# RWKV attention with two MLP blocks on one core: a prologue with one reciprocal table, a later broadcast of u, and other PSUM banks for the first chunks

## The chip, the cores and the metric

The kernel runs on one core of one Trainium2 chip. The metric is the device time of one execution in microseconds (us); lower is better. Three timed runs of the kernel before gave 740.57, 743.58 and 743.90 us, so the median is 743.58 us.

## The reference

Three stages follow one another on fp32 data: a linear attention with a decaying state (4 batches, 8 heads, 768 steps, head width 48), an MLP with squared ReLU (3072 tokens, 384 to 2048 to 384), and an MLP with a softmax-weighted activation, a layer norm and a projection (384 to 1024 to 384).

```python
for t in range(S):                       # S = 768, per batch and head
    cur = outer(u * k[t], v[t])          # 48 x 48
    y[t] = r[t] @ (state + cur)
    state = w[:, None] * state + outer(k[t], v[t])

x = y as (3072, 384)
h = maximum(x @ w_in, 0);   x = (h * h) @ w_out
h = x @ w2_in;  solu = h * softmax(h)
out = (solu - mean) / sqrt(var + 1e-6) * g_ln @ w2_out
```

## The kernel before

**Attention in chunks.** The 3072 tokens are cut into 24 chunks of 128; chunk c belongs to batch c % 4. Inside a chunk the recurrence is a masked matrix of scores. The decay is folded in by a table `pt` of powers of w from w^-64 to w^63 (`setup_tables`, L276): r is multiplied with the table, k with the table reversed, and then TensorE (PE) forms scores (L417), VectorE (DVE) copies the part above the diagonal into a tile `atw` (L466), whose diagonal GpSimd (POOL) has already filled from r, u and k (`prep_b`, L370 to L389), and PE multiplies with v (L533). The result y of the first four chunks stays in a PSUM bank until `split_x` (L553) turns it into a high part `xh` (ScalarE, ACT, L563) and a low part `xl` (DVE, L564).

**Split matmuls.** Every fp32 product of the two MLPs is done as three fp32r products: high by high, low by high, high by low. So each weight is split on chip after it has landed in a staging tile `stg`: three DVE instructions undo a 64-bit form (L584, L587, L590), ACT casts the high part (L602), POOL subtracts to get the low part (L603). There are 28 such units for the first MLP and six staging buffers.

**The first MLP.** A step is one tile of 128 hidden units: `p1` (L637) makes it from xh, xl and wih, wil in one of the banks 3 and 4, ACT squares it (L649 to L651), DVE makes the low part gl (L652), and `p2` (L655) adds it, through woh and wol, into the accumulators in banks 5, 6 and 7. A block is 512 tokens, that is four chunks; the first block is begun in halves of 256 tokens (steps 0 to 3 for chunks 0 and 1, steps 4 to 7 for chunks 2 and 3).

**The prologue.** Loads are issued by SyncE (SP) in program order (L825 to L834), with u, broadcast to 128 partitions, issued by ACT (L826). Then `setup_tables`, the first two chunks (L837 to L847), chunks 2 and 3 (L849 to L855), and `setup_ktab` (L317), which transposes two tables by PE through bank 7. The list `YB` at L836 says which bank each of the first chunks' y uses: 5, 6, 7 and 1. The scores of chunks 0, 2 and 3 go to banks 0 and 1, those of chunk 1 to banks 3 and 4.

**What sets the order.** A scheduler that simulates the program fixes the order of instructions on every engine; from then on each engine works through its own list in order and waits on semaphores. So an edit in the prologue also reorders later instructions. The program has eight completion semaphores for its loads, used in turn: the ninth load is issued when the first has landed.

Of the kernel before, what the change touches and what calls it, by code (L numbers as in the profile page):

```python
# [177 lines left out]
def rwkv_moe_moe2_kernel(ctx, tc, rkd, tok, tk2, wd, w, u, w_in, w_out, w2_in, w2_out, g_ln, out):  # L178
# [29 lines left out]
    pwr = ac.tile([GR, 8, NP], F32, name="pwr")  # L208
    ipw = ac.tile([GR, 8, NP], F32, name="ipw")
    kpt = ac.tile([128, DM], F32, name="kpt")  # L210
# [64 lines left out]

    def setup_tables():  # L276
        R = pt[:, 0]
        nc.vector.memset(R[:, :, HC:HC + 1], 1.0)
        nc.vector.tensor_scalar(out=pwr[:, 0], in0=wdt, scalar1=W_MIN, scalar2=W_MAX, op0=ALU.max, op1=ALU.min)
        n, s = 1, 0  # L280
        while n <= HC:
            if n < HC:
                nc.vector.tensor_tensor(out=pwr[:, s + 1], in0=pwr[:, s], in1=pwr[:, s], op=ALU.mult)
            nc.vector.reciprocal(ipw[:, s], pwr[:, s])
            if n == HC:
                nc.vector.tensor_copy(R[:, :, 0], ipw[:, s])
            else:
                for o, src, t in ((HC + n, HC, pwr), (HC + 1 - 2 * n, HC + 1 - n, ipw)):
                    nc.vector.tensor_tensor(
                        out=R[:, :, o:o + n],  # L290
                        in0=R[:, :, src:src + n],
                        in1=t[:, s].unsqueeze(2).to_broadcast([GR, NP, n]),
                        op=ALU.mult,
                    )
            n, s = 2 * n, s + 1
        nc.scalar.copy(pt[:, 1], R[:, :, ::-1])

# [19 lines left out]
    def setup_ktab():  # L317
        v = ps[:, 7, :].rearrange("p (a b) -> p a b", a=NP)
        for p in range(NP):
# [20 lines left out]
    def halves(t):  # L340
        return t.rearrange("q p (s i) -> q p s i", s=2)

    def prep_rk(c, eng=None):
        if c >= B:
            k = halves(rk_t[c])
            nc.gpsimd.tensor_tensor(out=k, in0=k, in1=sub_tab(pt[:, 1]), op=ALU.mult)
            for j in range(2):
                q = slice(RO[j], RO[j] + D)
                r = halves(mv[c % 2][q, j])
                nc.gpsimd.tensor_tensor(out=r, in0=r, in1=sub_tab(pt[q, 0]), op=ALU.mult)  # L350
        elif eng:
            eng.tensor_tensor(out=rk_t[c], in0=rk_t[c], in1=pt, op=ALU.mult)
        else:
            for p in range(0, NP, 2):
                for i, t in enumerate((pt[:, 0], pt[:, 0, :, ::-1])):
                    x = rk_t[c][:, i, p:p + 2]
                    nc.vector.tensor_tensor(out=x, in0=x, in1=t[:, p:p + 2], op=ALU.mult)
# [53 lines left out]

    def pe_scores(c, sb=0):
        rk = rk_t[c]
        if c < B:
            for h in range(H):
                o = RO[h % 2]
# [44 lines left out]

    def dve_mask(c, sb=0):
        if c < B:
            m = mask.bitcast(U32).unsqueeze(1).to_broadcast([C, NP, C])
            for i in range(2):
                nc.vector.copy_predicated(  # L466
# [358 lines left out]
    nc.sync.dma_start(out=wdt, in_=wd)  # L825
    nc.scalar.dma_start(out=ub, in_=u.unsqueeze(0).to_broadcast([128, DM]))  # L826
    load_chunk(0)
    w1_load()
    load_chunk(1)
# [5 lines left out]
    setup_tables()  # L835
    SB, YB = (0, 3, 0, 0), (5, 6, 7, 1)  # L836
    for c in range(2):  # L837
# [10 lines left out]
    setup_wm()  # L848
    for c in range(2, 4):  # L849
        prep_rk(c, nc.gpsimd)  # L850
        prep_b(c)
        pe_scores(c, SB[c])
        dve_mask(c, SB[c])
        pe_av_direct(c, YB[c])
        split_x(c)  # L855
    setup_ktab()
# [169 lines left out]
```

## Time and profile before

| | |
|---|---|
| Median of three runs | 743.58 us |
| Profiled execution, its own time | 740.04 us |
| Its span | 738.2 us |
| PE busy in the span | 707.3 us (96%) |
| DVE busy | 417.5 us (57%) |
| ACT, POOL busy | 322.1 us (44%), 268.2 us (36%) |
| Granted TensorE clock, mean | 0.984 of full speed |
| DMA | 62.72 MB, 85 GB/s mean |

The profile is of one execution, taken by the hardware profiler. Times in it count from the start of the span. A group of instructions is named by its engine, its line in the kernel, its operation, and output and inputs by tile name. "Idle before" is time in which the engine stood still just before the instruction, with what ended it behind an arrow. PE's two clock levels are 2.4 GHz (granted 1.00) and 1.2 GHz (granted 0.50). Most fp32 matmuls appear as two entries where they take two passes.

### The profile page before, as it was taken

What the parts mean: (1) busy time and instruction counts of PE and PEld (TensorE: products, weight loads), DVE (VectorE), ACT (ScalarE), POOL (GpSimd) and SP (SyncE); (2) the same over time, 40 slices, a digit from 0 to 9 for tenths busy, and PEclk for the clock granted to TensorE, in tenths of its full rate; (3) what the DMA queues carried; (4) which work ended last, traced back from release to release, by engine and by line L of the source; (5) the groups of instructions that cost most, each with busy time, mean ns of one, the idle gap of its engine ahead of it and who ended that gap; (6) DMA issues with size and microseconds to landing.
All of it is one profiled execution on the core that took longest, in us unless ns stands there. A gap on an engine that the chain in (4) does not pass through costs nothing.

```text
span 738.2 us, 13162 instructions
## 1 busy us (share of the span) xinstructions
PE 707.3 (96%) x5088; PEld 604.3 (82%) x5088; DVE 417.5 (57%) x764; ACT 322.1 (44%) x625; POOL 268.2 (36%) x297
## 2 busy tenths in 40 slices
PE   2699999899999999999999999999999999999996
PEld 2579777688888888888888888888899999999996
DVE  6879997444643333333332265714777767677771
ACT  1325566344545454544555455644424232322232
POOL 4978777515543333333332021722213120200000
PEclk9869999999999999999999999999999999999999
DMA  9946553313223222322143015320210100000001
GB/s 258 268 132 226 178 179 91 95 36 99 84 66 110 62 61 64 109 67 68 46 120 115 12 25 192 109 86 1 96 65 17 67 15 21 22 22 23 21 33 37
DMA packets 35112, 62.72 MB, mean 85 GB/s; under 512 B 7777, under 2 KB 17378, under 8 KB 35042
## 3 DMA queue, kind: packets, MB, share of 16 engines
q1 hardware_dynamic: 34898, 61.60, 27.0%
q8 instruction: 42, 0.69, 0.4%
q10 hardware_dynamic: 144, 0.20, 0.3%
q14 instruction: 28, 0.23, 0.1%
HBM read 48.41 MB, written 9.44 MB: 78 GB/s over the span
## 4 chain that ended last, share of the span: by engine, by line
PE 82%; DVE 6%; DMA 3%; issue 2%; POOL 2%; SPq 2%; ACT 2%; DVEq 0%; ACTq 0%; POOLq 0%
PE ps L644 8%; PE ps L645 8%; PE ps L662 7%; PE ps L663 7%; PE ps L646 7%; PE ps L666 7%; PE ps L812 5%; PE ps L811 5%; PE ps L814 5%; PE ps L748 4%; PE ps L750 4%; PE ps L749 4%; PE ps L795 3%; PE ps L507 2%; PE ps L430 2%
## 5 line engine op out<-in xcount | busy, mean ns | idle before, releaser
L652 DVE TENSOR_TENSOR gl<-ps,gh 128x512 fp32r<-128x512 f32 (+1 forms) x100 | 66.7, 667 | 173.6 <-ACT gh L651 173.5
L644 PE MATMUL ps<-xh,wih 128*128 128x512 f32 (+1 forms) x300 | 118.3, 396 | 3.8 <-ACT xh L563 2.1
L646 PE MATMUL ps<-xh,wil 128*128 128x512 f32 (+1 forms) x300 | 115.9, 387 | 2.7 <-POOL wil L603 2.7
L662 PE MATMUL ps<-gh,woh 128*128 128x512 f32 (+1 forms) x300 | 115.0, 386 | 1.4 <-ACT gh L651 1.4
L645 PE MATMUL ps<-xl,wih 128*128 128x512 f32 (+1 forms) x300 | 115.7, 386 | 0.5 <-DVE xl L564 0.5
L663 PE MATMUL ps<-gh,wol 128*128 128x512 f32 (+1 forms) x300 | 114.2, 383 | 0.3 <-POOL wol L603 0.3
L649 ACT ACTIVATE ps<-ps 128x512 f32<-128x512 f32 (+1 forms) x100 | 56.4, 565 | 115.9 <-PE ps L646 115.8
L350 POOL TENSOR_TENSOR mv<-mv,pt 48x512 f32<-48x512 f32 x40 | 52.8, 1321 | 90.2 <-DMA mv<-in_rkd_dram 89.8
L666 PE MATMUL ps<-gl,woh 128*128 128x512 f32 (+1 forms) x300 | 84.1, 383 | 0.4 <-DVE gl L652 0.4
L644 PEld LDWEIGHTS ps<-xh,wih 128*128 128x128 f32 x300 | 57.3, 191 | 16.4 <-ACT xh L563 2.4
L646 PEld LDWEIGHTS ps<-xh,wil 128*128 128x128 f32 x300 | 57.4, 192 | 14.3 <-POOL wil L603 2.9
L662 PEld LDWEIGHTS ps<-gh,woh 128*128 128x128 f32 x300 | 56.9, 190 | 13.4 <-ACT gh L651 2.0
L645 PEld LDWEIGHTS ps<-xl,wih 128*128 128x128 f32 x300 | 57.5, 192 | 11.3 <-DVE xl L564 1.2
L663 PEld LDWEIGHTS ps<-gh,wol 128*128 128x128 f32 x300 | 56.7, 190 | 11.6 <-POOL wol L603 0.5
L666 PEld LDWEIGHTS ps<-gl,woh 128*128 128x128 f32 x300 | 55.8, 190 | 11.7 <-DVE gl L652 0.9
L811 PE MATMUL ps<-w2oh,lth 128*128 128x384 f32 x192 | 65.1, 339 | 0.2 <-ACT lth L804 0.2
L812 PE MATMUL ps<-w2ol,lth 128*128 128x384 f32 x192 | 65.1, 339 | 0.0
L651 ACT CAST gh<-ps 128x512 fp32r<-128x512 f32 (+1 forms) x100 | 57.2, 572 | 4.3 <-PE ps L663 1.4
L650 ACT ACTIVATE ps<-ps 128x512 f32<-128x512 f32 (+1 forms) x100 | 56.5, 566 | 2.9
L748 PE MATMUL ps<-w2ih,xh 128*128 128x512 f32 x144 | 57.3, 398 | 0.0
L749 PE MATMUL ps<-w2il,xh 128*128 128x512 f32 x144 | 56.8, 395 | 0.0
L750 PE MATMUL ps<-w2ih,xl 128*128 128x512 f32 x144 | 56.7, 395 | 0.0
(121 smaller groups left out, 1192.3 us busy)
## 6 DMA issues: line engine op xcount, KB each, us to landing
stg<-in_w_in_dram SPq DMA_DIRECT2D x18, 512.0 KB, 5.9
stg<-in_w_out_dram SPq DMA_DIRECT2D x24, 384.0 KB, 3.7
tok<-in_tk_dram SPq DMA_DIRECT2D x20, 384.0 KB, 3.7
x2d<-stg SPq DMA_DIRECT2D x18, 256.0 KB, 2.5
x2r<-x2d SPq DMA_DIRECT2D x6, 768.0 KB, 5.0
out_dram<-ob SPq DMA_DIRECT2D x24, 192.0 KB, 1.9
kd<-in_rkd_dram SPq DMA_DIRECT2D x20, 224.0 KB, 3.8
mv<-in_rkd_dram SPq DMA_DIRECT2D x40, 96.0 KB, 2.3
```

The lines of the kernel that those rows point to most:

```text
L644: nc.tensor.matmul(hp, wih[g][:, k, f], xh[:, k, cs], start=(k == 0), stop=False)
L645: nc.tensor.matmul(hp, wih[g][:, k, f], xl[:, k, cs], start=False, stop=False)
L646: nc.tensor.matmul(hp, wil[g][:, k, f], xh[:, k, cs], start=False, stop=(k == KD - 1))
L652: nc.vector.tensor_tensor(out=gl, in0=hp, in1=gh.bitcast(F32), op=ALU.subtract)
L662: nc.tensor.matmul(acc[e], woh[m // 4][:, m % 4, f], gh, start=start, stop=False)
L663: nc.tensor.matmul(acc[e], wol[m // 4][:, m % 4, f], gh, start=False, stop=False)
L666: nc.tensor.matmul(acc[e], woh[m // 4][:, m % 4, f], gl, start=False, stop=stop)
L748: nc.tensor.matmul(o, x2h[j][:, k, s], w2["ih"][:, k, fs], start=(k == 0), stop=False)
L749: nc.tensor.matmul(o, x2h[j][:, k, s], w2["il"][:, k, fs], start=False, stop=False)
L750: nc.tensor.matmul(o, x2l[j][:, k, s], w2["ih"][:, k, fs], start=False, stop=(k == KD - 1))
L811: nc.tensor.matmul(o, hi[:, m], w2["oh"][:, m], start=(m == 0), stop=False)
L812: nc.tensor.matmul(o, hi[:, m], w2["ol"][m // 4][:, m % 4], start=False, stop=False)
```

## The change

Four things in the prologue are changed, and one tile goes.

1. The broadcast of u is issued by SP behind the two loads of chunk 0, not by ACT beside the first load.
2. The powers of w: the positive powers are still doubled step by step, but the negative ones are no longer built beside them from seven small reciprocals. Instead the whole negative half is one reciprocal of the positive half read backwards (63 powers of 4 head pairs), behind one of 4 elements.
3. The outputs y of chunks 2 and 3 move from banks 7 and 1 to banks 1 and 0, and the table transposes of `setup_ktab` from bank 7 to bank 1. Chunk 3's scores and masking are issued in two halves (even heads in bank 0, odd heads in bank 1), and chunk 2's output stands between them.
4. Chunks 2 and 3 are prepared together ahead of both chunks' scores, and POOL's table products for chunks 4 and 5 may not come before the last instruction of that preparation (`after_first`).

```diff
 def setup_tables():
-        while n <= HC:
-            if n < HC:
-                nc.vector.tensor_tensor(out=pwr[:, s + 1], in0=pwr[:, s], in1=pwr[:, s], op=ALU.mult)
-            nc.vector.reciprocal(ipw[:, s], pwr[:, s])
-            if n == HC:
-                nc.vector.tensor_copy(R[:, :, 0], ipw[:, s])
-            else:
-                for o, src, t in ((HC + n, HC, pwr), (HC + 1 - 2 * n, HC + 1 - n, ipw)):
...
+        while n < HC:
+            nc.vector.tensor_tensor(out=pwr[:, s + 1], in0=pwr[:, s], in1=pwr[:, s], op=ALU.mult)
+            nc.vector.tensor_tensor(
+                out=R[:, :, HC + n:HC + 2 * n],
+                in0=R[:, :, HC:HC + n],
+                in1=pwr[:, s].unsqueeze(2).to_broadcast([GR, NP, n]),
+                op=ALU.mult,
+            )
             n, s = 2 * n, s + 1
+        nc.vector.reciprocal(R[:, :, 0], pwr[:, s])
+        nc.vector.reciprocal(R[:, :, 1:HC], R[:, :, :HC:-1])

 def setup_ktab():
-        v = ps[:, 7, :].rearrange("p (a b) -> p a b", a=NP)
+        v = ps[:, 1, :].rearrange("p (a b) -> p a b", a=NP)

+    def after_first(c):
+        if c < B + 2:
+            tc.add_manual_dep(
+                nc.cur_bb.bb.instructions[-1], last_first.name,
+                mybir.DependencyInfo(mybir.DependencyClass.NoSync, mybir.DependencyReason.DATA),
+                reason="after_first",
+            )
 def prep_rk(c, eng=None):        # after_first(c) behind each of its three POOL products
...
-    nc.scalar.dma_start(out=ub, in_=u.unsqueeze(0).to_broadcast([128, DM]))
     load_chunk(0)
+    nc.sync.dma_start(out=ub, in_=u.unsqueeze(0).to_broadcast([128, DM]))
...
-    SB, YB = (0, 3, 0, 0), (5, 6, 7, 1)
+    SB, YB = (0, 3, 0, 0), (5, 6, 1, 0)
...
-    for c in range(2, 4):
-        prep_rk(c, nc.gpsimd)
-        prep_b(c)
-        pe_scores(c, SB[c])
-        dve_mask(c, SB[c])
-        pe_av_direct(c, YB[c])
-        split_x(c)
+    prep_rk(2, nc.gpsimd)
+    prep_b(2)
+    prep_rk(3, nc.gpsimd)
+    prep_b(3)
+    last_first = nc.cur_bb.bb.instructions[-1]
+    pe_scores(2)
+    dve_mask(2)
+    pe_scores(3, 0, range(0, H, 2))
+    pe_av_direct(2, YB[2])
+    split_x(2)
+    dve_mask(3, 0, (0,))
+    pe_scores(3, 0, range(1, H, 2))
+    dve_mask(3, 0, (1,))
+    pe_av_direct(3, YB[3])
+    split_x(3)
     setup_ktab()
```

On POOL, from the second table product for chunk 2 on, the order was (rkw holds r and k of chunks 2 and 3, tokw their token-major tiles, wil and wol the low weight parts):

```order
L352 TENSOR_TENSOR rkw<-rkw,pt 112x1024
L378 TENSOR_TENSOR tokw<-tokw,ub 128x384
L379 TENSOR_TENSOR tokw<-tokw 128x384
L603 TENSOR_TENSOR wil<-stg,wih 128x512
L379 TENSOR_TENSOR tokw<-tokw 128x384
L603 TENSOR_TENSOR wol<-stg,woh 128x384
L346 TENSOR_TENSOR kd<-kd,pt 112x512
L350 TENSOR_TENSOR mv_96<-mv_96,pt 48x512 x2
L385 AFFINE_SELECT atw<-b 128x1024
```

and it is now (L359 is the old L352, L385 and L386 the old L378 and L379, L610 the old L603, L392 the old L385, L351 and L356 the old L346 and L350):

```order
L359 TENSOR_TENSOR rkw<-rkw,pt 112x1024
L610 TENSOR_TENSOR wil<-stg,wih 128x512
L385 TENSOR_TENSOR tokw<-tokw,ub 128x384
L386 TENSOR_TENSOR tokw<-tokw 128x384
L610 TENSOR_TENSOR wol<-stg,woh 128x384
L386 TENSOR_TENSOR tokw<-tokw 128x384
L610 TENSOR_TENSOR wol<-stg,woh 128x384
L392 AFFINE_SELECT atw<-b 128x1024 x2
L351 TENSOR_TENSOR kd<-kd,pt 112x512
L610 TENSOR_TENSOR wol<-stg,woh 128x384
```

The third wil product stands two products earlier, and the two diagonals of atw stand ahead of all products for chunk 4 (kd, mv).

On PE, where steps 2 and 3 of the first block and chunks 2 and 3 stand, the order was (x2 in a p2 row: only banks 5 and 6 of the three accumulators):

```order
L663 MATMUL ps<-gh,wol 128x256 x2
L666 MATMUL ps<-gl,woh 128x256 x2
L533 MATMUL ps<-atw,tokw 64x128
L417 MATMUL ps<-rkw 128x128 x4
L662 MATMUL ps<-gh,woh 128x256 x2
L533 MATMUL ps<-atw,tokw 64x128 x5
L533 MATMUL ps<-atw,tokw 48x128 x6
L417 MATMUL ps<-rkw 128x128 x4
L663 MATMUL ps<-gh,wol 128x256 x2
L666 MATMUL ps<-gl,woh 128x256 x2
L320 MATMUL ps<-ident,pt 128x112 x4
```

and it is now (L670, L673, L669 are p2's old L663, L666, L662; L424 the old L417, L540 the old L533, L316 the old L320):

```order
L670 MATMUL ps<-gh,wol 128x256 x3
L673 MATMUL ps<-gl,woh 128x256 x3
L669 MATMUL ps<-gh,woh 128x256 x3
L424 MATMUL ps<-rkw 128x128 x4
L540 MATMUL ps<-atw,tokw 64x128 x6
L540 MATMUL ps<-atw,tokw 48x128 x6
L670 MATMUL ps<-gh,wol 128x256 x3
L673 MATMUL ps<-gl,woh 128x256 x3
L669 MATMUL ps<-gh,woh 128x256 x3
L540 MATMUL ps<-atw,tokw 64x128
L424 MATMUL ps<-rkw 128x128 x4
```

All three accumulators now go together, and the second half of chunk 3's scores stands behind chunk 2's output.

## Rows read from the trace of the kernel before

**Rows 1.** The page: span and instructions.

```profile
span 738.2 us, 13162 instructions
```

**Rows 2.** By stretch: us; busy PE, PEld, DVE, ACT, POOL; clock; DMA share; GB/s.

```profile
0.00:10.00 10.00, 0.00 (x0) 0.00 (x0) 3.64 (x32) 2.13 (x3) 4.07 (x19) 1.00 0.81 210
10.00:24.00 14.00, 9.77 (x79) 7.75 (x80) 13.93 (x22) 2.10 (x4) 9.82 (x9) 1.00 1.03 311
24.00:34.00 10.00, 5.03 (x40) 3.94 (x38) 8.01 (x16) 4.24 (x11) 10.00 (x9) 0.88 0.90 241
...
42.00:54.00 12.00, 12.00 (x90) 10.13 (x89) 8.84 (x17) 2.28 (x4) 8.07 (x7) 0.58 0.36 100
54.00:122.00 68.00, 66.28 (x671) 55.64 (x671) 62.89 (x113) 38.95 (x82) 53.59 (x51) 1.00 0.54 169
```

**Rows 3.** PE's waits up to 130 us: line, waited for, us, times, longest.

```profile
PE ps L417 <- DVE mv L357: 13.6, 4, 10.7
```

**Rows 4.** Timeline of DVE, 6 to 14 us: start, us, instruction, idle before.

```profile
6.35 0.17 DVE L279 TENSOR_SCALAR pwr<-wdt 112x4 f32<-112x4 f32 x1 [5.42 <-DMA wdt<-in_wd_dram]
...
9.12 3.03 DVE L357 TENSOR_TENSOR mv<-mv,pt 112x256 f32<-112x256 f32 x4
...
12.68 0.54 DVE L383 TENSOR_REDUCE b<-tok 128x8 f32<-128x384 f32 x1
...
13.73 0.93 DVE L357 TENSOR_TENSOR mv<-mv,pt 112x256 f32<-112x256 f32 x1
```

**Rows 5.** DVE by line and shape, 6 to 9.3 us: busy us, mean ns.

```profile
L284 DVE RECIPROCAL ipw<-pwr 112x4 f32<-112x4 f32 x7 | 1.2, 168 | 0.0
...
L289 DVE TENSOR_TENSOR pt<-pt,ipw 112x128 f32<-112x128 f32 x1 | 0.3, 282 | 0.0
```

**Rows 6.** DVE by line and shape, 650 to 720 us.

```profile
L775 DVE RECIPROCAL sm<-z 128x1 f32<-128x1 f32 x8 | 1.3, 156 | 0.0
```

**Rows 7.** Tile mv up to 35 us: ns min/median/max, first and last start.

```profile
L357 DVE TENSOR_TENSOR mv<-mv,pt x8: 409/1066/1218, 9.1 to 16.9; 112x256 f32<-112x256 f32 x8
```

**Rows 8.** DMA queue of u in the first 5 us: packets, MB, engines' share.

```profile
q10 hardware_dynamic: 138, 0.19, 38.6%
```

**Rows 9.** DMA issues at 0.80, 1.73, 2.20 and 2.67 us: KB, us to landing.

```profile
wdt<-in_wd_dram SPq DMA_DIRECT2D x1, 1.8 KB, 5.5
...
tok<-in_tok_dram SPq DMA_DIRECT2D x1, 576.0 KB, 7.4
...
stg<-in_w_in_dram SPq DMA_DIRECT2D x1, 512.0 KB, 9.0
...
mv<-in_rkd_dram SPq DMA_DIRECT2D x1, 448.0 KB, 10.2
```

**Rows 10.** The page, DMA issues of the output, median us to landing.

```profile
out_dram<-ob SPq DMA_DIRECT2D x24, 192.0 KB, 1.9
```

**Rows 11.** Timeline of POOL, 29 to 31 us.

```profile
29.13 1.01 POOL L379 TENSOR_TENSOR tokw<-tokw 128x384 f32<-128x384 f32 x1
30.09 1.30 POOL L603 TENSOR_TENSOR wil<-stg,wih 128x512 fp32r<-128x512 f32 x1
```

**Rows 12.** Timeline of PE, around 31 to 34 and 58 us.

```profile
31.45 0.60 PE L646 MATMUL ps<-xh,wil 128*128 128x256 f32 x2 [2.69 <-POOL wil L603]
33.41 0.58 PE L662 MATMUL ps<-gh,woh 128*128 128x256 f32 x1 [1.37 <-ACT gh L651]
...
58.42 0.28 PE L645 MATMUL ps<-xl,wih 128*128 128x256 f32 x1
58.54 0.28 PE L646 MATMUL ps<-xh,wil 128*128 128x256 f32 x1
```

**Rows 13.** Timeline of DVE between 37 and 55 us.

```profile
37.83 0.69 DVE L584 TENSOR_SCALAR ps<-stg 128x512 uint32<-128x512 uint32 x1 [1.65 <-DMA stg<-in_w_in_dram]
...
40.23 1.33 DVE L466 COPY_PREDICATED atw<-mask,ps 128x512 f32<-128x512 uint32 x2
...
54.03 0.56 DVE L564 TENSOR_TENSOR xl<-ps,xh 128x384 fp32r<-128x384 f32 x1
```

More of the change, by code (lines that the diff above doesn't have):

```diff
@@ L208, in rwkv_moe_moe2_kernel @@
     pwr = ac.tile([GR, 8, NP], F32, name="pwr")
-    ipw = ac.tile([GR, 8, NP], F32, name="ipw")
     kpt = ac.tile([128, DM], F32, name="kpt")
@@ L280, in setup_tables @@
         n, s = 1, 0
-        while n <= HC:
-            if n < HC:
-                nc.vector.tensor_tensor(out=pwr[:, s + 1], in0=pwr[:, s], in1=pwr[:, s], op=ALU.mult)
-            nc.vector.reciprocal(ipw[:, s], pwr[:, s])
-            if n == HC:
-                nc.vector.tensor_copy(R[:, :, 0], ipw[:, s])
-            else:
-                for o, src, t in ((HC + n, HC, pwr), (HC + 1 - 2 * n, HC + 1 - n, ipw)):
[L289 to L294, printed above, removed]
+        while n < HC:
[6 more added lines that the diff above has]
+            )
             n, s = 2 * n, s + 1
+        nc.vector.reciprocal(R[:, :, 0], pwr[:, s])
+        nc.vector.reciprocal(R[:, :, 1:HC], R[:, :, :HC:-1])
         nc.scalar.copy(pt[:, 1], R[:, :, ::-1])
@@ L346, in prep_rk @@
             nc.gpsimd.tensor_tensor(out=k, in0=k, in1=sub_tab(pt[:, 1]), op=ALU.mult)
+            after_first(c)
             for j in range(2):
@@ L350, in prep_rk @@
                 nc.gpsimd.tensor_tensor(out=r, in0=r, in1=sub_tab(pt[q, 0]), op=ALU.mult)
+                after_first(c)
         elif eng:
@@ L410, in put_state, with pe_scores @@
             nc.scalar.copy(vs[c % 2][q, j, s], sg[c % B][q])
-    def pe_scores(c, sb=0):
+    def pe_scores(c, sb=0, heads=range(H)):
         rk = rk_t[c]
         if c < B:
-            for h in range(H):
+            for h in heads:
                 o = RO[h % 2]
@@ L460, in pe_u, with dve_mask @@
                     ))
-    def dve_mask(c, sb=0):
+    def dve_mask(c, sb=0, js=range(2)):
         if c < B:
             m = mask.bitcast(U32).unsqueeze(1).to_broadcast([C, NP, C])
-            for i in range(2):
+            for i in js:
                 nc.vector.copy_predicated(
```

## Prediction

> **What bounds the kernel now.** I read the page first, then the busy time by stretch, then PE's waits, and last the timelines of the engines that the waits name, with the DMA landings beside them. The span is 738.2 us [rows 1] and the execution took 740.04 us, so 1.8 us lie around the span. In the stretch from 54 to 122 us PE is busy 66.28 of 68 us, and DVE, which converts weights there, 62.89 [rows 2]: both are nearly full. The first 54 us are different. PE does nothing for 10 us, 9.77 us in the next 14 and 5.03 in the 10 behind; and from 42 to 54 it is busy throughout, but at a granted clock of 0.58 [rows 2], mostly at 1.2 GHz. So the change works where there is something to get, and the question is how much of an earlier start lives through the full stretch behind it.
>
> PE's largest wait, 13.6 us, is for chunk 0's and 1's products with the table on DVE [rows 3]. They start at 9.12 us, behind tables that begin when wdt lands at 6.35 [rows 4]. But other things arrive late as well, and most of the working below is about which of them comes next.
>
> **The change part by part.**
>
> *The broadcast of u.* In the first 5 us u's queue holds 38.6% of 16 engines, 31 engine-us for 0.19 MB [rows 8], and the 1.8 KB of wdt take 5.5 us beside it [rows 9]. Without u in front, wdt cannot land before 0.80 + 1.9 = 2.7 us (the fastest group of issues [rows 10]) nor, if u was not what held it, before 6.3. I take 4.0, nearer to the short end because wdt is so small.
>
> *The tables.* Before, 29 DVE instructions run from 6.35 to 9.12, 0.095 us from start to start [rows 4]. Now there are 16 of them, 1.5 us, and one reciprocal of 252 elements, whose cost no row shows. From below: a product of 128 elements takes 0.28 us [rows 5], so some 0.4 us. From above: a reciprocal takes 156 ns for one element [rows 6] and 168 ns for four [rows 5], 4 ns more each, so 0.17 + 248 x 0.004 = 1.2 us. I take 1.2, since that comes from reciprocals. The tables are then done at 4.0 + 1.5 + 1.2 + 0.2 = 6.9 us instead of 9.12; in themselves they are hardly shorter than before (2.9 against 2.8).
>
> Those bounds say nothing of how the chip divides. The Trainium skill does ("VectorE: DVE Perf Modes", the walkthrough of the 8-slice pipeline): a reciprocal is an iterated divide with a repeat count of 8. Read as eight cycles per element at that page's 0.96 GHz, 252 elements would be 2.1 us (an estimate from the page). The measured 4 ns per element are about half of that, so the trace neither confirms nor excludes it; by it the tables would end at 7.8.
>
> *Chunk 0.* Its four products take 3.03 us [rows 4] because POOL works on tok beside them; one alone takes 0.41 [rows 7]. POOL now waits for u, so I take 4 x 0.41 = 1.6 and end at 8.5 instead of 12.1. But the next instruction of DVE's list, L584, needs the first weight load, issued at 2.20 and landed 9.0 later, at 11.2 [rows 9]. The bytes ahead of it are the same ones in another order, so it lands at 11.2 again, and L383 behind it starts at 11.8 instead of 12.68: 0.9 us are left of 3.6. L383 also needs POOL, and POOL needs u. Up to u the queue now carries what it carried up to chunk 0's tok, which landed at 1.73 + 7.4 = 9.1 [rows 9], so POOL starts at about 9.3 as before and its two products (1.0 us each, as L379 in [rows 11]) are done at 11.4. If u's 31 engine-us come on top undivided (1.9 us on each of 16 engines), L383 starts at 13.2, 0.5 later than before. I keep this as the poor end.
>
> *Chunk 1.* Its mv lands at 2.67 + 10.2 = 12.9 [rows 9], its products started at 13.73 [rows 4]: at most 0.8 us. With a little less mixing with POOL I carry 1.0 us of lead into POOL's list.
>
> *POOL and the first step.* From 24 to 34 us POOL is busy 10.00 of 10 us [rows 2], and PE's first step waits 2.69 us for the third wil product, which ends at 31.4 behind products for chunks 2 and 3 [rows 11, 12]. The new order puts it ahead of one L378 and one L379, of 1.0 us each [rows 11]. So PE's L646 goes from 31.45 to 31.45 - 2.0 - 1.0 = 28.4. ACT has one more weight cast (0.5 us) in front of its gh, so p2 of step 0 goes from 33.41 [rows 12] to 31.0: 2.4 us of lead.
>
> *The banks.* Before, bank 7 was taken by chunk 2's y and by the table transposes, so the third accumulator's matmuls of steps 0 to 2 stood behind all this, and steps 1 to 3 stayed half open. Now steps 1 to 3 run through between 31 and 39 us (39 matmuls of 256 columns, 0.12 us apart at 2.4 GHz [rows 12], twice that at 1.2). Behind them DVE sets the pace, and at 37.83 it waits for a weight load [rows 13]. The loads ahead of this one are unchanged, so it lands at 37.8 again. What DVE gains there is what it has done before it: chunk 2's two masks, 1.3 us of DVE's time [rows 13], and a gl, so some 1.5 us.
>
> From there to chunk 3's xl there is now a chain: even scores, mask, chunk 2's y, its xh and xl out of bank 1, odd scores into bank 1, mask, chunk 3's y, xh, xl, with two to three weight instructions of 0.7 us in DVE's list between. Adding the durations I get xl at 46 us with PE at 2.4 GHz and at 50 with PE at 1.2; before it was 54.03 [rows 13]. Of the work that stood ahead of xl, 3.9 us of DVE's now stand behind it, so DVE leads by 54.0 - 48 - 3.9 = 2.1 us (0.1 to 4.1). PE ends p1 of step 5 after 16 more matmuls (1.9 to 3.8 us), at 50 to 53.8; before, this was at 58.8 [rows 12], of which 1.0 us were matmuls that now come later. PE leads by 4 to 8 us.
>
> *What is left at 122 us.* p1 writes banks 3 and 4 in turn, and the bank is free only when DVE has made gl, so PE can't run away from DVE. DVE idles 68 - 62.89 = 5.1 us in this stretch [rows 2]. A part of that is waiting for loads that PE's own matmuls release, which come earlier now; I take 2.1 us of it. So the lead at 122 us is 2.1 + 2.1 = 4.2 us. Behind it DVE has little to do, and the lead stays.
>
> The new DMA issue on SP (0.4 us) and the extra waits inside the chain are in these sums; the removed tile costs nothing.
>
> **The sum.** 740.04 - 4.2 = 735.8 us against the profiled execution. The median of the runs stands 3.5 us above it, so 743.58 - 4.2 = 739.4 us is the forecast.
>
> **The rivals.**
> - *PE's lead survives.* If DVE takes up all of its 5.1 idle us on top of its 2.1, PE keeps 7 to 8 us: 736. For it: PE is ahead by 4 to 8 and what DVE waits for comes earlier. Against it: DVE is at 92% [rows 2], and a list worked through in order never fills completely.
> - *The loads hide it.* If u costs the queue its 1.9 us, if wdt is not earlier and the reciprocal is dear (1.2 us or more), the head starts no sooner, and only the moved masks are left: 1.5 us, so 742. For it: three of the marks above (11.2, 12.9, 37.8) are landings. By the Trainium skill's iterated divide (the page and section above) the tables would end at 9.9 with wdt at 6.3, which is this case and no worse, as L584 waits until 11.2 anyway.
> - *The new chain is slower.* Bank 1 carries chunk 3's odd scores only after chunk 2's xl, bank 0 its y only after both masks. If DVE's list holds each of the three hops behind three weight instructions (2.1 us instead of 1.4) and PE stands meanwhile, xl comes at 54 or later and nothing is gained; if the clock then falls for another 10 us, as it did after 42 us (0.58 over 12 us is 10 us at half [rows 2]), half of them are lost: 743.6 + 5 - 1.2 for the earlier accumulators = 747. It decides at xl = 54 us. Against it: my dear case ends at 50.
>
> PE stood for the 2.69 and 1.37 us of [rows 12] before the clock first fell. The Trainium skill ("TensorE: Matmul & The Clock Gate", Part 1) says that the low clock is the resting state and that sustained activity releases it. The rows agree; by it the new idle places, at about 27, 30 and 43 us, can cost a fall each, which is why the last rival is not smaller.
>
> **How the numbers follow.** Forecast 0.47 (739.4, own range 737 to 742), PE's lead 0.25 (736), loads 0.20 (742), slower 0.08 (747). Leaving out two in ten, the range is 734 to 743.5: down to a lead of 9.6, the whole of PE's and some, up to no gain. A difference under 0.5%, 3.7 us, is about what a measurement of this kernel cannot tell from none. Faster by more: 0.6 of the forecast, nearly all of the PE case, a little of the loads, 0.54. Slower by more: part of the last, 0.05. Within: 0.41.
>
> **What would show it.** Right: wdt lands near 4 us and the products start before 8; L584 waits for its load until about 11; the first step's last matmul is near 28.4; L584 waits again at 37 to 38; chunk 3's xl is at 46 to 50. Wrong: wdt at 6 still; POOL waiting for u past 10; xl at 54; a stretch at half clock beyond 53 us; PE idle for DVE in 54 to 122 us by as much as it was early.

## The result, and the profile after

The changed kernel took 732.01 us (median of four runs) against 743.29 us for the kernel before beside it: ratio 0.9846 [0.9811, 0.9881]. In a second comparison it took 729.55 us against 741.15: 0.985 [0.982, 0.988]. Over all runs that list a clock (10 and 81) the means are 730.8 and 740.8 us, 10.0 us apart. The forecast was 739.4, its range 734 to 743.5: right in sign, and its 4.2 us are less than half of the 11.3 between the medians or the 10.0 between the means.

The profiled execution took 732.05 us. The page's span, and the stretches that answer to [rows 1, 2], with the same columns:

```profile
span 730.3 us, 13143 instructions
```

```profile
0.00:10.00 10.00, 2.08 (x16) 1.78 (x16) 5.64 (x23) 2.52 (x3) 5.24 (x20) 1.00 0.77 225
10.00:24.00 14.00, 10.58 (x86) 8.33 (x87) 13.22 (x23) 2.75 (x5) 11.49 (x10) 1.00 1.02 342
24.00:34.00 10.00, 7.03 (x53) 6.31 (x51) 6.28 (x13) 4.75 (x13) 10.00 (x10) 1.00 0.83 211
34.00:42.00 8.00, 5.90 (x44) 5.11 (x45) 7.61 (x14) 2.34 (x5) 7.69 (x7) 0.79 0.74 266
42.00:54.00 12.00, 10.96 (x119) 9.79 (x120) 10.59 (x25) 6.26 (x16) 5.87 (x6) 1.00 0.57 182
54.00:122.00 68.00, 64.88 (x640) 52.01 (x639) 62.03 (x108) 38.55 (x80) 55.62 (x53) 0.97 0.53 160
```

The stretch from 42 to 54 us ran at 0.58 before and runs at 1.00 now (at 0.86 in the second profile of the changed kernel, which its repeat below left). Between 34 and 42 us, a stretch that [rows 2] leaves out, the clock is low in both kernels. The kernel before:

```profile
34.00:42.00 8.00, 6.76 (x36) 6.18 (x36) 6.01 (x11) 2.94 (x8) 7.70 (x8) 0.71 0.72 250
```

From 54 to 122 us PE waits more than before (64.88 busy against 66.28) and the clock falls once (0.97): the changed kernel is early there, and its longest waits are for products of POOL and DVE (1.3 and 1.0 us).

DVE's head, to be held against [rows 4]:

```profile
2.46 0.47 DVE L279 TENSOR_SCALAR pwr<-wdt 112x4 f32<-112x4 f32 x1 [1.53 <-DMA wdt<-in_wd_dram]
...
4.68 1.72 DVE L291 RECIPROCAL pt<-pt 112x252 f32<-112x252 f32 x1
6.43 1.43 DVE L364 TENSOR_TENSOR mv<-mv,pt 112x256 f32<-112x256 f32 x4
9.76 0.70 DVE L591 TENSOR_SCALAR ps<-stg 128x512 uint32<-128x512 uint32 x1 [1.89 <-DMA stg<-in_w_in_dram]
10.36 0.54 DVE L390 TENSOR_REDUCE b<-tok 128x8 f32<-128x384 f32 x1
...
11.51 2.68 DVE L364 TENSOR_TENSOR mv<-mv,pt 112x256 f32<-112x256 f32 x4
```

wdt lands at 2.4 us instead of 6.3 (forecast 4.0). The reciprocal of 252 elements is dear, 1.72 us (forecast 1.2), but chunk 0's products, 1.43 instead of 3.03 us, start at 6.43 (forecast 6.9). Then DVE waits for the first weight load (L591, the old L584), as foretold; only it comes at 9.76, not at 11.2. PE's wait for these products [rows 3] and its first steps [rows 12]:

```profile
PE ps L424 <- DVE mv L364: 10.9, 3, 7.2
```

```profile
26.47 0.50 PE L653 MATMUL ps<-xh,wil 128*128 128x256 f32 x2 [1.08 <-POOL wil L610]
28.85 0.62 PE L669 MATMUL ps<-gh,woh 128*128 128x256 f32 x3 [1.87 <-ACT gh L658]
```

31.45 has become 26.47 (forecast 28.4) and 33.41 has become 28.85 (forecast 31.0); in the second profile they are 27.75 and 30.24. The marks on DVE that answer to [rows 13]:

```profile
35.33 1.34 DVE L473 COPY_PREDICATED atw<-mask,ps 128x512 f32<-128x512 uint32 x2
...
37.22 0.69 DVE L591 TENSOR_SCALAR ps<-stg 128x512 uint32<-128x512 uint32 x1 [0.26 <-DMA stg<-in_w_in_dram]
...
46.45 0.55 DVE L571 TENSOR_TENSOR xl<-ps,xh 128x384 fp32r<-128x384 f32 x1
```

Chunk 2's masks come 4.9 us earlier, chunk 3's xl 7.6 us earlier (54.03 to 46.45; forecast 46 to 50; 48.36 in the second profile). Each of DVE's copies of a finished block (L671, now L678) is a further mark. Block 0's starts at 127.26 us instead of 132.71, a lead of 5.45; block 1's at 215.50 instead of 223.27, 7.8. From there to the end both kernels take 514.8 to 514.9 us. So in this pair everything is decided before block 1 ends, and 2.3 us of it between the two copies, where the forecast had nothing.

### The profile page after: what moved, and what is told of

It reads as the page before. It is cut to its first block, busy times and chain, and to the rows that moved or that the text cites. A ratio compares the mean times of both kernels' runs of the same rounds, so it can differ in the third digit from the quotient of the medians.

```text
span 730.3 us, 13143 instructions
## 1 busy us (share of the span) xinstructions
PE 702.9 (96%) x5088; PEld 599.7 (82%) x5088; DVE 418.7 (57%) x752; ACT 321.7 (44%) x625; POOL 267.9 (37%) x297
## 4 chain that ended last, share of the span: by engine, by line
PE 86%; DMA 7%; SPq 2%; POOL 2%; ACT 1%; issue 1%; DVE 0%; ACTq 0%; POOLq 0%; DVEq 0%
PE ps L651 9%; PE ps L653 8%; PE ps L652 8%; PE ps L670 8%; PE ps L669 8%; PE ps L673 8%; PE ps L819 5%; PE ps L818 5%; PE ps L821 5%; PE ps L755 5%; PE ps L757 5%; PE ps L756 5%; DMA stg<-in_w_out_dram 3%; PE ps L802 3%; PE ps L514 2%; PE ps L437 2%
## 5 line engine op out<-in xcount | busy, mean ns | idle before, releaser
L669 PE MATMUL ps<-gh,woh 128*128 128x512 f32 (+1 forms) x300 | 113.3, 383 | 2.2 <-ACT gh L658 2.1
L670 PE MATMUL ps<-gh,wol 128*128 128x512 f32 (+1 forms) x300 | 113.3, 383 | 0.0
L356 POOL TENSOR_TENSOR mv<-mv,pt 48x512 f32<-48x512 f32 x40 | 52.1, 1302 | 93.0 <-DMA mv<-in_rkd_dram 92.3
L673 PE MATMUL ps<-gl,woh 128*128 128x512 f32 (+1 forms) x300 | 83.3, 382 | 0.0
L669 PEld LDWEIGHTS ps<-gh,woh 128*128 128x128 f32 x300 | 56.0, 189 | 13.9 <-ACT gh L658 2.9
L670 PEld LDWEIGHTS ps<-gh,wol 128*128 128x128 f32 x300 | 56.1, 189 | 11.2 <-issue 0.4
L673 PEld LDWEIGHTS ps<-gl,woh 128*128 128x128 f32 x300 | 55.7, 189 | 10.9
L827 ACT COPY ob<-ps 128x384 f32<-128x384 f32 x24 | 11.5, 480 | 102.9 <-issue 81.2
```

Source lines behind the costliest of these rows:

```text
L669: nc.tensor.matmul(acc[e], woh[m // 4][:, m % 4, f], gh, start=start, stop=False)
L670: nc.tensor.matmul(acc[e], wol[m // 4][:, m % 4, f], gh, start=False, stop=False)
L673: nc.tensor.matmul(acc[e], woh[m // 4][:, m % 4, f], gl, start=False, stop=stop)
```

## The experiments

**How the runs are read.** Every run lists its span and its mean granted clock. Span times (1 - clock) is the time lost to the low clock, span times clock is the rest. In 81 runs the kernel before loses 9.15 us (0.9876) and has 729.9 of rest; in ten runs the changed kernel loses 4.8 (0.9934) and has 724.2. So 4.3 of the 10.0 us go with the clock and 5.7 with the rest. This is accounting; whether the clock is a cause is tested further below. In the table, lost and rest are means of all runs of a kernel; the ratio is to the kernel before on the same chip. A difference between two kernels given with +- is one of the means of all their runs, with twice its standard error.

| Kernel | Runs | Median us | Ratio [95%] | Lost to clock | Rest |
|---|---|---|---|---|---|
| before | 81 | 740.8 | | 9.15 | 729.9 |
| changed | 10 | 730.8 | 0.985 [0.982, 0.988] (six of them) | 4.8 | 724.2 |
| u's move alone | 12 | 737.9 | 0.9960 [0.9938, 0.9983] | 9.2 | 726.6 |
| tables alone | 12 | 741.5 | 1.0014 [0.9986, 1.0042] | 9.6 | 730.1 |
| order and banks alone | 9 | 734.2 | 0.9939 [0.9914, 0.9964] | 6.85 | 726.5 |
| changed, u in front | 9 | 735.1 | 0.9940 [0.9918, 0.9962] | 4.7 | 728.6 |
| changed, old tables | 6 | 732.3 | 0.9878 [0.9847, 0.9909] | 5.2 | 725.4 |
| changed, bank 7 | 6 | 734.4 | 0.9907 [0.9879, 0.9934] | 6.7 | 725.8 |
| changed, no after_first | 12 | 737.1 | 0.9961 [0.9937, 0.9985] | 7.9 | 728.1 |
| before, PE filled | 12 | 738.4 | 0.9965 [0.9943, 0.9988] | 6.1 | 730.75 |
| changed, u from 128 rows | 5 | 734.1 | 0.9905 [0.9873, 0.9938] | 5.0 | 727.3 |
| changed, masks ahead | 12 | 738.5 | 0.9960 [0.9939, 0.9982] | 7.6 | 729.3 |
| masks ahead, u by PE | 6 | 735.2 | 0.9922 [0.9893, 0.9951] | 4.9 | 728.7 |
| changed, PE filled | 6 | 729.6 | 0.9853 [0.9810, 0.9895] | 3.3 | 724.7 |
| changed, u by PE | 6 | 731.5 | 0.9876 [0.9832, 0.9919] | 4.1 | 725.3 |
| u by PE, PE filled | 6 | 729.6 | 0.9868 [0.9824, 0.9912] | 2.8 | 725.5 |

### The three parts, one at a time

u's broadcast alone, in the kernel before:

```diff
-    nc.scalar.dma_start(out=ub, in_=u.unsqueeze(0).to_broadcast([128, DM]))
     load_chunk(0)
+    nc.sync.dma_start(out=ub, in_=u.unsqueeze(0).to_broadcast([128, DM]))
```

> The kernel before with one line moved: u's broadcast is issued on SP behind chunk 0's loads. Theory A (two sources that add: an earlier load stream, and a clock that does not fall): wdt lands near 2.5 us, the first weight load near 9.8 instead of 11.2 (where DVE's L584 stops waiting, 12.08 before), but the tables still take 2.8 us, the order and the banks are those of before, so the first step's last matmul comes at about 30 us and the clock still falls; 2 to 3 us faster than before, about 741 against a median of 743.3. Theory B (the clock alone): the head is hidden behind the old order, nothing is gained, 743. Theory C (u was the whole cost): 735 or less.

Measured 737.9, theory A: 3 us, nearly all of it in the rest (-2.8 against the runs beside it). wdt lands at 2.5 and L584 stops waiting at 9.80; the first step's last matmul comes at 28.37 (about 30 was expected), chunk 3's xl at 52.29.

The new `setup_tables` alone (that part of the diff as it stands):

> The kernel before with the new tables alone; u's broadcast stays in front on ACT. Theory A: wdt still lands at 6.3 us, the tables take 4.0 us (16 small instructions and one reciprocal of 1.7 us) instead of 2.8, so chunk 0's products start at about 10 instead of 9.12, and L584 waits for its load until 12 anyway: within 1 us of before, 743. Theory B says the same. A rival on the tables: fewer DVE instructions leave POOL's port free earlier and the time falls by 1 us or more.

Measured no difference; chunk 0's products start at 9.25 us instead of 9.12. The new order and the banks alone (points 3 and 4 of the change):

> The kernel before with the new banks and the new order of chunks 2 and 3 alone. Theory A: the first step's last matmul comes 1 to 2 us earlier (POOL's wil product is ahead of two products for chunk 3), chunk 3's xl at about 49 instead of 54, the stretch at the low clock is shorter than the 17 us of before: 4 to 6 us faster than before, 738. Theory B: the clock stays high as in the changed kernel and all of the gain is here, 732 to 733. Theory C: without the earlier head the chain of banks 0 and 1 gains nothing, 743 or more.

Measured 734.2. Against the runs beside it the clock gives 2.5 and the rest 3.0: theory A, at the upper end. Its mark on the first step failed (30.96, only 0.5 us earlier); chunk 3's xl comes at 48.40. The whole change but with u's broadcast back in front:

> The changed kernel with one line put back: u's broadcast in front on ACT. Theory A: the head is 1.3 to 2.5 us later (wdt 6.3, tables done at 10, L591 waits until 12), the first step's last matmul near 29, 2 to 3 us slower than the changed kernel, 734.5. Theory B: the clock behaves as in the changed kernel, within 1 us of it, 732 to 733. Theory C: nearly all is lost, 740 or more.

Measured 735.1: 4.3 +- 1.6 us slower than the changed kernel; the scatter does not tell this from the 3 us that the move brings alone. The parts alone sum to -3.0 + 0.8 - 5.5 = -7.7 us of the 10.0. That sum is uncertain by some 3 us, so it is not shown that the parts bring more together than alone. The same kernel once more beside others gave 729.55:

> The changed kernel once more, beside the other kernels of this call. If the parts add (u alone 3 us, order alone 5 to 6, tables nothing, from the runs above), it stands 8 to 9 us under the kernel before, near 732.5. If the first comparison (11.3 us between the medians) was the kernel itself and the kernel before was not only caught high, 11 us.

That is 11.6 us under the kernel before by the medians and 10.6 by the means, nearer to the second expectation.

### Inside the order: the bank and POOL's list

Chunk 2's y and the table transposes back in bank 7:

```diff
-        v = ps[:, 1, :].rearrange("p (a b) -> p a b", a=NP)
+        v = ps[:, 7, :].rearrange("p (a b) -> p a b", a=NP)
-    SB, YB = (0, 3, 0, 0), (5, 6, 1, 0)
+    SB, YB = (0, 3, 0, 0), (5, 6, 7, 0)
```

> The changed kernel with chunk 2's y and the table transposes put back into bank 7, the third accumulator's bank; the new order of chunks 2 and 3 stays. Theory A (the bank is what lets steps 1 to 3 run through, and what PE does there early is not to be done later): the third accumulator's nine matmuls for the first three steps come behind the table transposes again, about 1.0 us of PE's time at 46 to 50 us and a gl of DVE's; chunk 3's xl still near 46 to 47; 1 to 2 us slower than the changed kernel. Theory B (the order of DVE's and POOL's lists is all of it): within 0.7 us of the changed kernel. Theory C (the bank is all of it): 5 us slower.

Measured 3.4 +- 1.8 us slower, between A and C. The dependency on POOL away:

```diff
     nc.gpsimd.tensor_tensor(out=k, in0=k, in1=sub_tab(pt[:, 1]), op=ALU.mult)
-    after_first(c)
... (its definition and its other call go too)
```

> The changed kernel without the dependency that holds chunk 4's and 5's products on POOL behind chunk 2's and 3's. Theory A: in POOL's list the first wil products stand as in the changed kernel and chunk 4's products stand one to three places earlier, behind the first step: first step's last matmul near 26.5 as in the changed kernel, within 1 us of it. Theory D (POOL's list is what brings the gain): one POOL product of 1 us ahead of a wil or wol product, 2 us or more slower.

Measured 7.0 +- 1.6 us slower: my theory A was wrong, and of the edits that take one item away this costs most. The trace shows where it begins. POOL's timeline of the kernel before, then of this kernel (L342, L346, L381 here), then of the changed one:

```profile
33.28 1.28 POOL L346 TENSOR_TENSOR kd<-kd,pt 112x512 f32<-112x512 f32 x1
34.64 2.63 POOL L350 TENSOR_TENSOR mv<-mv,pt 48x512 f32<-48x512 f32 x2
37.23 1.08 POOL L385 TENSOR_SCALAR_AFFINE_SELECT atw<-b 128x1024 f32<-128x1024 f32 x1
...
41.98 1.09 POOL L385 TENSOR_SCALAR_AFFINE_SELECT atw<-b 128x1024 f32<-128x1024 f32 x1
```

```profile
29.04 1.32 POOL L342 TENSOR_TENSOR kd<-kd,pt 112x512 f32<-112x512 f32 x1
...
31.42 2.63 POOL L346 TENSOR_TENSOR mv<-mv,pt 48x512 f32<-48x512 f32 x2
...
36.23 1.08 POOL L381 TENSOR_SCALAR_AFFINE_SELECT atw<-b 128x1024 f32<-128x1024 f32 x1
```

```profile
31.25 2.13 POOL L392 TENSOR_SCALAR_AFFINE_SELECT atw<-b 128x1024 f32<-128x1024 f32 x2
33.36 1.27 POOL L351 TENSOR_TENSOR kd<-kd,pt 112x512 f32<-112x512 f32 x1
```

Chunk 4's products, 3.9 us on POOL that nobody needs yet, stand ahead of chunk 2's diagonals in the first two lists (in the second, chunk 5's kd at 34.98 too) and behind both chunks' in the third. DVE's masks write into these diagonals, so without the dependency the masks start at 39.38 and chunk 3's xl at 53.44, nearly as before, although the first step is as early as in the changed kernel (26.27). The lists behind 54 us differ too, so how much of the 7.0 us the diagonals alone cost is not shown.

### What makes u's broadcast dear, and what its move is worth

The changed kernel with u in front, but read from 128 different rows:

```diff
-    nc.scalar.dma_start(out=ub, in_=u.unsqueeze(0).to_broadcast([128, DM]))
+    nc.scalar.dma_start(out=ub, in_=tok[5, :, 0])
```

> The changed kernel with the broadcast back in front on ACT (as in the run with u in front), but reading 128 different rows of tok instead of one row of u 128 times: the same bytes and packets; the output is not the reference's, since u is replaced. If the repeated row is what makes that transfer slow (31 engine-us for 0.19 MB before), its queue takes a few engine-us, wdt lands at 2.5 to 3.5 us instead of 5.8, and the first weight load about 1 us earlier than with u in front (L591 stops waiting near 11). If it is the second queue in front, or its 128 packets, that delays the others, wdt still lands near 5.8.

DMA issues with u in front (first), and from 128 rows (second): KB, us to landing.

```profile
ub<-in_u_dram ACTq DMA_DIRECT2D x1, 192.0 KB, 4.8
wdt<-in_wd_dram SPq DMA_DIRECT2D x1, 1.8 KB, 5.0
```

```profile
ub<-in_tok_dram ACTq DMA_DIRECT2D x1, 192.0 KB, 2.6
wdt<-in_wd_dram SPq DMA_DIRECT2D x1, 1.8 KB, 2.8
```

The repeated row it is: the same bytes on the same queue land 2.2 us earlier, and wdt with them (the source is also another tensor, which no run separates). The first weight load, issued at 2.20 in both, takes 6.6 us to land instead of 8.8. These two kernels have the same instruction lists on PE, DVE and POOL, so they also tell what the head alone is worth. DVE's first conversion starts at 9.99 instead of 12.14, and the time falls by 1.0 +- 1.5 us. The changed kernel has about the same head (9.76 and 10.63 in its two profiles) and is another 3.3 +- 1.7 us faster. From 22 us on its lists are others. So, by elimination, much of what u's move brings beside the other parts is not the early load but the other list that the scheduler wrote for it.

u loaded once (1.5 KB) and spread by PE:

```diff
+    nc.sync.dma_start(out=urow, in_=u.unsqueeze(0))
...
+    nc.tensor.matmul(ps[:, 6, :DM], ones, urow, start=True, stop=True)
+    nc.scalar.copy(ub, ps[:, 6, :DM])
...
-    nc.sync.dma_start(out=ub, in_=u.unsqueeze(0).to_broadcast([128, DM]))
```

> The changed kernel with u loaded once (1.5 KB) and spread by a matmul with ones, without the other ordering dependency of the last pair. If that spreading brought the 3.3 us by which it beat its partner in the last pair, it brings them here too: 727 to 728. If what decides is the list that the scheduler writes for 54 to 122 us, which changes with each edit, it can come out anywhere between 728 and 735, although the head is 0.5 to 1 us earlier.

0.4 +- 1.8 us slower than the changed kernel: behind chunk 0's loads the transfer costs the end nothing that can be measured, though without it the first conversion starts at 8.58 us. The lists differ here too.

### Old tables, and one more dependency

The changed kernel with the old `setup_tables`:

> The changed kernel with the old tables (seven small reciprocals). The tables take 2.9 us instead of 4.0, chunk 0's products start near 5.6 instead of 6.4; but L591 behind them waits for its weight load until 9.8 in both. The forecast's view and theory A: within 0.7 us of the changed kernel. Rival: the tables are half of what u's move gains (u alone brought 3 us, u on top of tables and order 5 to 6): 2 to 3 us slower than the changed kernel.

1.6 +- 1.8 us slower: not told from no change, the rival not excluded. Chunk 0's products started at 6.16 there, waiting for their data, against 6.43, so the new tables themselves bring the head nothing.

The changed kernel with a dependency that holds one conversion behind chunk 2's masks:

```diff
+        if conv_n[0] == 7:   # the seventh conversion's first instruction
+            tc.add_manual_dep(nc.cur_bb.bb.instructions[-1], mask_c2.name, ...)
```

> The changed kernel with one more ordering dependency: the seventh weight conversion on DVE (L591, which waits 2.69 us for its load until 33.66) stands behind chunk 2's masks, which are ready at 32 us. Theory A (DVE's list and PE's wait for chunk 2's masks set the pace at 30 to 46 us): the masks run in DVE's idle time, PE's wait at 34 us goes from 2.12 to near 0, chunk 3's xl comes 1 to 2 us earlier, 1 to 2 us faster than the changed kernel. Theory B (the stretch behind, full of weight conversions, takes this back): within 0.7 us.

Both theories failed: 7.8 +- 1.7 us slower. Chunk 3's xl did come earlier, at 45.70, and the lead was then lost in the stretch behind. That stretch, PE's longest wait in it and DVE's:

```profile
54.00:122.00 68.00, 59.46 (x580) 47.24 (x579) 59.26 (x104) 34.94 (x71) 53.87 (x51) 0.94 0.54 166
```

```profile
PE ps L660 <- DVE gl L668: 3.9, 1, 3.9
```

```profile
DVE b L397 <- POOL tok L386: 5.3, 4, 3.4
```

PE is busy 59.46 us of 68, against 64.88 in the changed kernel: the scheduler wrote another list for these 68 us too, and in it DVE waits for POOL's products four times. Of the 7.8 us, 2.7 go with the clock. One edit at 33 us changed the order, and with it the waits, as far as 120 us. With u by PE on top:

> As the run before it, and u is loaded once (1.5 KB) and spread over the partitions by a matmul with ones and an ACT copy, so that the 0.19 MB transfer is gone. If this transfer still costs the load stream about its 1.9 us (31 engine-us over 16 engines) behind chunk 0's loads, the first weight load lands near 8.5 instead of 9.8 to 10.6 and the time falls by another 1 to 2 us. If it costs nothing there, the time is that of the run before it.

3.3 +- 1.4 us faster than its partner, but alone (above) the same edit brought nothing, so it is not the transfer by itself. By the accounting 2.7 of the 3.3 go with the clock and 0.6 with the rest; that the list is the reason is likely, not shown.

### Is the clock a cause?

The kernel before with PE's waits filled:

```diff
+            if i == 0 and k == KD - 1:
+                fill(22, 5, True)      # ahead of the last wil matmuls
+            if i == 1 and k == KD - 1:
+                fill(11, 5, True)      # ahead of step 0's first woh matmul
+            if i == 1 and e == 1:
+                fill(8, 5, False)      # behind step 1's gl matmuls
```

> The kernel before with added matmuls that fill PE's idle time ahead of the first low stretch of the clock: 22 of 256 columns before the first steps' last wil matmuls (where PE waits 2.69 us), 11 before step 0's first woh matmul (1.37 us), 8 behind step 1's gl matmuls at 40 us; those last ones add to an accumulator, so the output is not the reference's. Theory A (the low clock costs little, since DVE's list sets the pace there): the granted clock stays at 1.00 until about 40, the time is within 1.5 us of before. Theory B (the low clock from 32 to 38 and from 42 to 52 us is what the order removed): 3 to 5 us faster than before, although PE does more.

Its stretches (us; busy PE; clock; DMA share; GB/s), and PE's wait behind them:

```profile
24.00:34.00 10.00, 9.28 (x78) 1.00 0.82 228
34.00:42.00 8.00, 2.95 (x22) 0.89 0.73 247
```

```profile
41.58 0.69 PE L533 MATMUL ps<-atw,tokw 128*64 128x128 f32 x2 [4.98 <-DVE atw L466]
```

The clock stays high past 34 us, and what PE gains it spends waiting 4.98 us for chunk 2's masks; chunk 3's xl comes at 54.21, as before. There the low clock had cost nothing. Yet over all runs 3.0 us less are lost to the clock, the rest is 0.8 more, and the time falls by 2.2 +- 1.1 us (against the runs beside it 2.5 less, 0.1 more and 2.5 +- 1.4). Both theories hold half; where in the other executions the gain lies, one profile does not tell.

The changed kernel, and then the one with u by PE, filled in the same way:

```diff
+                fill(9, 5, True)       # ahead of the last wil matmuls
+                fill(15, 5, True)      # ahead of step 0's first woh matmul
+                fill(12, 5, False)     # zeros, behind step 1's gl matmuls
```

> The changed kernel with added matmuls in three of PE's waits: 9 where it waits 1.08 us for wil, 15 where it waits 1.87 us for gh (both into an accumulator that is started afresh behind them) and 12 with a zero operand where it waits 2.12 us for chunk 2's masks. Theory F (the clock's falls in the first 122 us cost the end what they take from PE, as the kernel before gained 2.5 us when filled): the granted clock rises from 0.993 to about 0.996, 2 us faster than the changed kernel, 728 to 729. Theory A (DVE's list sets the pace, the clock follows from its waits): the clock rises but the time is within 0.7 us of the changed kernel's 730.8.

> The run before it with the added matmuls of the changed kernel's filled version (the third group stands at another place here, behind 3 of its matmuls, since the list differs). Theory F: 2 us faster than the run before it. Theory A: within 0.7 us of it.

These fall by 1.0 +- 1.9 and 1.1 +- 1.8 us with 1.5 and 1.35 us less lost and 0.5 and 0.2 more rest. Neither difference stands by itself. No version beats the changed kernel by more than can be measured.

The 81 runs of the kernel before say something too, since their lists are all the same: from run to run the time grows by 0.73 +- 0.17 us for each us lost to the clock. Nine of them had a clock of 0.992 or more (mean 0.9928), and they took 738.3 us on average, where the changed kernel takes 730.8 at 0.9934. So some 7.5 of the 10.0 us are left at a like clock. A run that waits longer for another reason may also lose its clock, so this is a correlation; but the filled kernel before, 2.2 us faster for 3.0 less lost, has the same proportion. I take the clock as a cause of some 2 to 3 of the 10.0 us.

The kernel before, profiled again:

> The kernel before, unchanged, profiled once more. Theory E (the forecast's last step fell: the lead does not simply stay behind 122 us, since PE waits for chunk 7 at the end of block 0 and the clock can fall there): block 0's result is copied within 2 us of 132.7, and the stretch from there to block 1's copy is again 88 to 91 us, against 87.4 to 88.5 in the runs with the new order. Rival: the fall of the clock at 137 us in the first profile was a single accident, and this profile has none in any stretch behind 122 us and 86 to 87 us between the two copies.

741.79 us. Block 0's copy is at 135.69 (not within 2 us) and the stretch to block 1's is 88.65 us, within 88 to 91. PE's timeline at the end of block 0 in the first profile of before, and in the one of after:

```profile
135.98 0.73 PE L644 MATMUL ps<-xh,wih 128*128 128x512 f32 x2 [1.28 <-ACT xh L563]
...
138.34 0.63 PE L645 MATMUL ps<-xl,wih 128*128 128x512 f32 x1
138.76 0.63 PE L646 MATMUL ps<-xh,wil 128*128 128x512 f32 x1
```

```profile
130.22 0.73 PE L651 MATMUL ps<-xh,wih 128*128 128x512 f32 x2 [0.97 <-ACT xh L570]
...
131.14 0.39 PE L653 MATMUL ps<-xh,wil 128*128 128x512 f32 x1
131.37 0.39 PE L651 MATMUL ps<-xh,wih 128*128 128x512 f32 x1
```

Both wait there for chunk 7's xh. In before the clock then falls (0.42 us from matmul to matmul instead of 0.23), for 3 to 4 us; from this first matmul to block 1's copy it takes 87.3 us, in after 85.3, which is 2.0 of the 2.3 us found between the copies. The second profile of before has no fall there, but 0.93 from 54 to 80 us; it loses 9.6 us in all. So the fall is not tied to that place. In the second pair, this profile and the repeat of the changed kernel, the stretch between the copies is 1.3 us shorter (88.65 to 87.38) with no fall in either, so the clock is not all of that gain; and behind block 1's copy they take 515.8 and 514.8 us, another 1.0. Most of the difference in clock lies earlier. From 30 to 54 us, the two profiles of before, then the two of the changed kernel:

```profile
30.00:54.00 24.00, 19.95 (x127) 17.20 (x127) 18.13 (x34) 7.90 (x19) 19.77 (x18) 0.64 0.55 169
30.00:54.00 24.00, 17.70 (x127) 15.29 (x127) 16.87 (x30) 7.40 (x19) 18.28 (x16) 0.72 0.58 177
30.00:54.00 24.00, 20.85 (x195) 18.69 (x195) 19.51 (x41) 10.62 (x26) 17.56 (x16) 0.93 0.67 216
30.00:54.00 24.00, 21.23 (x175) 19.36 (x176) 19.09 (x39) 9.45 (x23) 18.06 (x16) 0.86 0.63 203
```

That is 8.6 and 6.7 us lost to the clock against 1.7 and 3.4.

## Why the prediction was wrong

The mechanism was right in sign and order: wdt first, then L584 at its load, POOL's wil, the banks, xl at 46 to 50. The step from there to the end failed in size, and one term was missing.

- **The failed step** is "What is left at 122 us": a lead of 2.1 + 2.1 = 4.2, and "Behind it DVE has little to do, and the lead stays." The two pairs of profiles show 5.45 and 5.8 us at the end of block 0 and 7.8 and 7.1 at the end of block 1. That was so although the second profile's xl, 48.36, is the very one of the forecast. From 12 us up to block 0's copy DVE runs the same instructions in both kernels, in another order, so both terms of the 4.2 can be read: the stretch from 54 us to that copy, first pair (before, changed), then second pair:

```profile
54.00:132.71 78.71, 75.96 (x738) 62.96 (x737) 67.29 (x122) 44.67 (x95) 60.17 (x57) 1.00 0.51 160
54.00:127.26 73.26, 70.14 (x663) 56.18 (x661) 63.18 (x110) 39.86 (x82) 59.27 (x57) 0.98 0.51 154
54.00:135.69 81.69, 77.66 (x738) 64.20 (x737) 68.48 (x125) 44.92 (x95) 59.33 (x57) 0.98 0.51 154
54.00:129.87 75.87, 71.95 (x689) 57.94 (x688) 64.12 (x115) 41.54 (x86) 60.81 (x57) 0.98 0.51 158
```

- **DVE's lead, forecast 2.1, was 4.1 and 4.4 us** (67.29 - 63.18, 68.48 - 64.12). This is the term that was too small. The other, the idle time that DVE takes up, was 1.3 and 1.5 for 2.1 (11.42 to 10.08, and 13.21 to 11.75).
- **Where DVE's lead came from** is known in part. "The bytes ahead of it are the same ones in another order, so it lands at 11.2 again" failed: L591 stopped waiting at 9.76 and 10.63 us in the two profiles, since the broadcast of one row holds up the loads behind it longer than its bytes say (8.8 us to landing behind u's row, 6.6 behind 128 rows). And on POOL I counted one L378 and one L379, 2.0 us; the list in front of me also had chunk 4's kd and mv go behind the diagonals, 3.9 us, and taking that dependency away costs 7.0 us. How the 2.0 to 2.3 us more divide between the two is open.
- **The missing term is the clock.** The sum 740.04 - 4.2 took the clock of one execution as given. The ten runs lose 4.3 us less to it than the 81, worth some 2 to 3 us at the end by the runs above, and the forecast has no term for that: it let the clock between 30 and 54 us move xl, not the end.
- **The start of the sum.** 743.58, a median of three runs, stood 2.8 us above the mean of the 81. That shifted the forecast's time, not its lead.
- **The tables.** The reciprocal was mis-sized, 1.72 us for 1.2, and the 16 small instructions took 2.2 for 1.5, without effect. The reciprocal takes 6.8 ns per element (1.72 us over 252). The Trainium skill ("VectorE: DVE Perf Modes", the walkthrough of the 8-slice pipeline) has the divide repeat eight times; the 2.1 us estimated from it are 0.4 too long, where my 1.2 from 4 ns per element were 0.5 too short.
- **The rivals.** "PE's lead survives" (736) has nearly the profile's number, 7.9 us, but not its way, so that number is luck. PE's last p1 matmul of step 5 came at 49.55 instead of 58.54, 8.0 us ahead when counted as the forecast does, without the 1.0 us of matmuls that come later. (Its early bound of 50 does not follow from xl at 46 and 1.9 us of matmuls, which give 47.9.) PE gave back 2.6 by the end of block 0 and got 2.3 back at the block's end, in that pair mostly by a clock that did not fall. "The loads hide it" fell with the 9.76; "the new chain is slower" with xl at 46.45.
- **The clock, as the last rival had it.** In the kernel before the clock fell between the two waits that the prediction names, behind the 2.69 us and ahead of the 1.37 (0.85 from 31 to 32 us, 0.50 from 32 to 33), not behind both. PE waits in the changed kernel too (1.08, 1.87 and 2.12 us). In its first profile the first two cost no fall and the clock fell behind the third (0.61 from 38 to 42 us); in the second it was 0.57 from 30 to 34 us and 0.79 from 42 to 50, near two of the places named. The Trainium skill ("TensorE: Matmul & The Clock Gate", Part 1) says that sustained activity releases the high clock; the filled kernel before agrees (mean 0.988 to 0.992).

What stays open: how much of the gain beside the clock the edits bring by themselves, and how much by the list that the scheduler happened to write behind them. The pair with equal lists gives 1.0 us for 2.2 us of head; the masks' dependency lost 7.8 although xl came earlier. A kernel with the changed kernel's list and u in front was not tried.

## What to carry to other kernels

Where a scheduler writes the lists, read the new lists over the whole full stretch behind an edit, and on every engine: what nobody needs yet and stands in front can cost more than the edit brings. Compare mean granted clocks beside the times, and make the sum against several executions, since a kernel that waits less may also lose less to the clock. A dependency that only orders one engine's list can be worth as much as a bank or a load: taking it away cost 7.0 +- 1.6 us here, the bank 3.4 +- 1.8, u's move 4.3 +- 1.6.

## What the runs showed of the hardware

- A broadcast of one 1.5 KB row to 128 partitions took 4.7 to 5.3 us to land in front of the other loads, the same 192 KB from 128 rows of another tensor 2.6 us. Its queue held 18 to 39% of 16 engines in the first 5 us, against 13%.
- One kernel's executions differ by up to 10.5 us (735.99 to 746.49, before) at mean granted clocks of 0.981 to 0.995, with 0.73 +- 0.17 us of time for each us lost to the clock; where the clock falls changes from one profile to the next.
- A reciprocal of 112x252 fp32 elements took 1.72 us on DVE, 6.8 ns per element, where one of 112x4 took 0.17.
